# Summing w_mod products over the partitions on VectorE (32x32 transposes and row sums) instead of with matmuls against ones

## The chip, the cores and the metric

The kernel runs on one core of one Trainium2 chip. The metric is the device time of one execution in microseconds; lower is better. A core has a matmul engine (TensorE, PE in the profile), a vector engine (VectorE, DVE), an activation engine (ScalarE, ACT), GpSimd (POOL) and a queue that issues most of the transfers (SP). The engines run side by side and wait for one another by semaphores. On-chip memory has 128 partitions; VectorE works along a row of each partition, and a matmul sums over the partitions.

## What is computed

One transformer block: linear attention (32 heads of 32) and a gated feed-forward part, both behind a layer norm that is modulated by a vector `c`. Cut to what matters here:

```
mod = silu(c) @ w_mod                      # c: 1024 values, w_mod: 1024 x 6144, bf16
sa, ca, ga, sb, cb, gb = six slices of 1024 of mod
h = layernorm(x) * (1 + ca) + sa
x = x + ga * A(h, wqkv, wo)                # linear attention, x is 2048 x 1024
h = layernorm(x) * (1 + cb) + sb
x = x + gb * (gelu(h @ w_gate) * (h @ w_up)) @ w_down
```

The change touches `ga` (gate of the attention), `sb` and `cb` (shift and scale of the second layer norm) and `gb` (gate of the feed-forward part): 4 x 1024 values. `sa` and `ca` are made in another way at the start and stay as they are.

## The kernel before

**Stages.** The program builds a list of operations for each engine in program order. In the profile, the first 26 us load data and make the first layer norm; to 127 us the k and q products run (L919, L970); from 127 to 192 us 24 tiles of the attention's summary matrix ("m tiles", L934, 16 matmuls each, 2.32 us a tile); to some 255 us the output projection (L1304); then the feed-forward part (L1475) to 601 us and its down projection (L1688) to the end.

**Order.** PE and SP run in the order in which the program is written. For the operations between the last k products of the first chunks and the second layer norm (about 27 to 205 us), a planner, `reorder`, gives DVE, ACT and POOL an order of their own: it takes a cost for each operation from the table `COST` (duration and latency, by name), works a due time back from what needs the result, and fills each engine with the ready operation that is due first. The resulting order is fixed when the program runs; each engine waits for its next operation's inputs, whatever else would be ready.

**The w_mod products.** Slices of 512 columns are handled one after another, k = 0 to 7: 0 and 1 are `ga`, 2 to 5 are `sb` and `cb`, 6 and 7 are `gb`. For each, DVE multiplies eight blocks of 128 rows of w_mod by the matching values of silu(c) and adds them up (`mod_acc`, L855 and L858; `gb_acc`, L833 and L835): one accumulator of 128 x 512 f32. Slices alternate between two accumulators; 6 shares the one of 0, 2 and 4. What is left is a sum over the 128 partitions:

- `mod_hi` (ACT, L864 and L842) rounds the accumulator to bf16, `mod_lo` (DVE, L868 and L843) takes the difference to the unrounded value, also in bf16;
- `mod_rows` (PE, L880, shown in the profile as L879) multiplies both parts by a block of ones, 128 x 32, in eight matmuls, four column groups side by side, and adds them in PSUM;
- `mod_store` (ACT, L886) copies the row to on-chip memory, and SP stores it to a scratch row in DRAM (L888): four packets;
- SP loads it back where it is needed: `ga` to all partitions (`gab`, L894), which DVE then folds into W_o (`wofold`, L1241); `sb` and `cb` as columns (`sbT`, `cbT`, L1252); `gb` to all partitions much later.

`ga_pass` does this behind m tile 0, `mod_pass` behind tile 14, `gb_rows` behind tile 21.

**What stands around it.** Behind certain m tiles the program inserts the next steps (`HOOK`): `kv_prod` (PE, L952, eight short matmuls, then DVE's masked copy `kvt`, L956), which needs a DMA transpose `mtb<-mb` of the finished summary rows (`m_t`, L735, issued by SP); `w2_pair` (PE, L1235), which needs `kvt` and the folded W_o; `den` (PE, L1262), then on DVE an addition, a reciprocal and a cast (L1267 to L1269), a store on SP (L1271), loads (L1283) and the scaling of q (L1296). den0's store stands on SP behind the loads of `sbT` and `cbT` and ahead of the transpose for kv4.

Of the kernel before, what the change touches and what calls it, by code (L numbers as in the profile page):

```python
# [189 lines left out]
class Sched:  # L190
# [41 lines left out]
    def dma(self, stream, fn, rd=(), wr=(), deps=(), note="", overwrite_ok=False):  # L232
# [6 lines left out]
        if prev is not None:  # L239
# [11 lines left out]
        DVE_: {"min": (0.34, 0.085), "add": (0.607, 0.085), "bn": (0.603, 0.085), "aggr": (0.124, 0.085), "ve": (0.07, 0.085), "xhat": (0.46, 0.085),  # L251
               "nm": (0.074, 0.085), "hmod": (0.25, 0.085), "macc": (0.66, 0.085), "mlo": (0.6, 0.085), "kvt": (0.21, 0.085), "z": (0.34, 0.085),
               "dene": (0.335, 0.085), "rden": (1.67, 0.085), "pqs": (0.62, 0.085), "wofold": (1.13, 0.085), "x": (1.14, 0.085), "ssum": (1.15, 0.085), "tsum": (1.15, 0.085), "padd": (0.62, 0.085), "yT": (0.62, 0.085)},
# [96 lines left out]
def bass_adaLN_cond__linear_attn_block__geglu_ffn__prompt_kernel(  # L350
# [18 lines left out]
    with ExitStack() as es:  # L369
# [6 lines left out]
        def at(name, shape, dty, off):  # L376
            return nc.alloc_sbuf_tensor_at(name, shape, dty, offset=ABASE + off, align_bytes=4)
# [44 lines left out]
        GBB = at("gbb", [P, D], f32, OFF_GBB)  # L422
        MROW = [at(f"mrow{i}", [P, 512], f32, OFF_ROW + i * 2048) for i in range(2)]
        MROW0 = at("mrowa", [P, 256], f32, XHO[2])
        WMG = [at(f"wmg{i}", [P, 4, 512], bf16, HBO[3] + i * 4096) for i in range(2)]
        MRG = at("mrg", [P, 256], f32, OFF_TMP + 4096)
        HLG = at("hlg", [P, 2, 2, 512], bf16, OFF_TMP)
        GAC = at("gacc", [P, 512], f32, OFF_TMP + 4096)
        ACC = [at(f"acc{i}", [P, 512], f32, OFF_ROW + i * 2048) for i in range(2)]
        HLO = OFF_WS + 16384  # L430
        HL = at("hl", [P, 4, 2, 512], bf16, HLO)
        KVT = at("kvt", [P, NG, P], bf16, OFF_KVT)
# [6 lines left out]
        for name, shape, dty, sz in [  # L439
            ("ident", [P, P], bf16, 256), ("bmask", [P, P], bf16, 256), ("bm32", [P, NG, NH], bf16, 512),   # L440
            ("z32", [P, NG, NH], bf16, 512), ("rdc", [P, SGW // 2], f32, 1024), ("rdh", [P, SGW // 2], bf16, 512),
            ("ones", [P, 32], bf16, 64), ("silf", [P, NDC], f32, 64),
            ("c8", [NDC, P], bf16, 256), ("cT", [P, NDC], f32, 64), ("chalf", [P, NDC], f32, 64),
            ("thc", [P, NDC], f32, 64), ("siluT", [P, NDC], bf16, 64), ("modt", [P, 16], f32, 64), ("add4", [P, 4], f32, 64),
            ("sbT", [P, NDC], f32, 64), ("cb1T", [P, NDC], f32, 64),
            ("cbT", [P, NDC], f32, 64), ("zcols", [P, NG], f32, 64), ("neghalf", [P, 1], f32, 64),
            ("st", [P, NCH, 12], f32, NCH * 48), ("mv", [P, NCH, 2], f32, NCH * 8),
            ("rs", [P, NCH], f32, 64), ("nm", [P, NCH], f32, 64), ("ve", [P, NCH], f32, 64),
        ]:
# [7 lines left out]
        ONES, SILF, C8, CT, CHALF, THC, SILUT = (_small[k] for k in ("ones", "silf", "c8", "cT", "chalf", "thc", "siluT"))  # L457
        SBT, CB1T, CBT, ZCOLS = (_small[k] for k in ("sbT", "cb1T", "cbT", "zcols"))
# [4 lines left out]
        def r_sm(name):  # L463
            return [(SMO[name], SMO[name] + SMSZ[name], name)]
# [69 lines left out]
        def r_wm(i, d0=0, d1=NDC):  # L534
            return [(MSO[i] + d0 * 1024, MSO[i] + d1 * 1024, f"wmst{i}")]

        def r_hl(k, h0, h1):
            return [(HLO + (2 * (k % 4) + h0) * 1024, HLO + (2 * (k % 4) + h1) * 1024, "hl")]

# [129 lines left out]
        sch.op(V, lambda e: e.tensor_copy(SILF[:, :], SILUT[:, :]), rd=r_sm("siluT"), wr=r_sm("silf"))  # L669
        sch.op(V, lambda e: e.memset(ONES[:, :], 1.0), wr=r_sm("ones"))  # L670

# [153 lines left out]

        def r_hlg(j, h):
            return [(OFF_TMP + (2 * j + h) * 1024, OFF_TMP + (2 * j + h + 1) * 1024, "hlg")]

        def gb_acc(j, dc):
# [9 lines left out]

        def gb_hilo(j):  # L840
            acc, rng = GA_[j]
            sch.op(A, lambda e: e.activation(HLG[:, j, 0, :], acc[:, :], ACTF.Copy), rd=rng, wr=r_hlg(j, 0), note=f"mhi{6 + j}")  # L842
            sch.op(V, lambda e: e.tensor_tensor(HLG[:, j, 1, :], acc[:, :], HLG[:, j, 0, :], ALU.subtract), rd=rng + r_hlg(j, 0), wr=r_hlg(j, 1), note=f"mlo{6 + j}")  # L843

        o_gb = [None]

        def gb_rows():
            mod_rows(((0, 2, 5, lambda j, h: (HLG[:, j, h, :], r_hlg(j, h))),))
            o_gb[0] = mod_store(2, 5, MRG, [(OFF_TMP + 4096, OFF_TMP + 5120, "mrg")], 2)

# [10 lines left out]

        def mod_hi(k):
            rng = r_2k(OFF_ROW + k % 2 * 2048, f"acc{k % 2}")
            sch.op(A, lambda e: e.activation(HL[:, k % 4, 0, :], ACC[k % 2][:, :], ACTF.Copy), rd=rng, wr=r_hl(k, 0, 1), note=f"mhi{k}")  # L864

        def mod_lo(k):
            rng = r_2k(OFF_ROW + k % 2 * 2048, f"acc{k % 2}")
            sch.op(V, lambda e: e.tensor_tensor(HL[:, k % 4, 1, :], ACC[k % 2][:, :], HL[:, k % 4, 0, :], ALU.subtract),  # L868
                   rd=rng + r_hl(k, 0, 1), wr=r_hl(k, 1, 2), note=f"mlo{k}")

        def mod_rows(parts):
            for k0, n, bank, src in parts:
                o = None
                w = n * P
                for h in range(2):
                    for j in range(4):
                        ap, rng = src(k0 + j * n // 4, h)
                        ap = ap[:, j * w % 512:j * w % 512 + w]
                        o = sch.op(T, lambda e, h=h, j=j, ap=ap, bank=bank, w=w: e.matmul(  # L879
                            ps_all[32 * j:32 * (j + 1), bank * 512:bank * 512 + w], ONES[:, :], ap, start=(h == 0), stop=(h == 1)),  # L880
                            rd=rng + r_sm("ones"), pwr=(pr(bank) if h == j == 0 else ()), note=f"modr{k0}.{h}.{j}")
                pset_writer(bank, o)

        def mod_store(n, bank, dst, rng, row):
            w = n * P
            sch.op(A, lambda e: e.activation(dst[:, 0:w], ps_all[:, bank * 512:bank * 512 + w], ACTF.Copy),  # L886
                   prd=pr(bank), wr=rng, note=f"mrow{row}")
            return sch.dma(Q, lambda e: e.dma_start(scr_row[row, 0:n, :].rearrange("a (h b) -> (a h) b", b=w), dst[0:128:32, 0:w]), rd=rng, note=f"mrow{row}.st")  # L888

        def hl_src(k, h):  # L890
            return HL[:, k % 4, h, :], r_hl(k, h, h + 1)

# [354 lines left out]
        def mod_pass():  # L1247
            assert mdone[0] >= 48 and not late
            mod_rows(((2, 4, 5, hl_src),))
            o_r = mod_store(4, 5, MROW[1], r_2k(OFF_ROW + 2048, "mrow1"), 1)  # L1250
            for dst, nt, a0 in ((SBT, "sbT", 0), (CBT, "cbT", 2)):
                sch.dma(Q, lambda e, dst=dst, a0=a0: e.dma_start(dst[:, :], scr_row[1, a0:a0 + 2, :].rearrange("a (b p) -> p (a b)", p=P)),  # L1252
                        wr=r_sm(nt), deps=[o_r], note=nt)

# [72 lines left out]
        def hook_run(f):  # L1327
# [754 lines left out]
```

## Time and profile before

| what | value |
|---|---|
| three runs | 784.52, 784.8, 785.14 us; median 784.8 |
| profiled execution | 784.59 us, of which the profile's span is 782.8 |
| PE busy | 771.0 us, 98% |
| DVE busy | 646.2 us, 83% |
| ACT busy | 352.7 us, 45% |
| granted PE clock | 1.0 in all forty slices |

The profile gives, for each engine, when it was busy; the chain of waits follows the work that ended last back from the end, step by step, to what released it. An engine that is busy for a large share of the span need not set the time: only the steps on the chain do.

| operation touched | engine, line | count | mean ns |
|---|---|---|---|
| round the accumulator to bf16 | ACT L864, L842 | 8 | 622 to 632 |
| difference, bf16 | DVE L868, L843 | 8 | 678 to 693 |
| matmul with ones, 512 columns | PE L879 | 8 | 385 |
| matmul with ones, 256 columns | PE L879 | 16 | 278 |
| row copy out of PSUM | ACT L886 | 3 | 378, 592, 383 |
| row store | SP L888 | 3 | issue 521 to 647 |

Matmuls are pipelined, so the mean time of one is longer than its distance from the next.

### The profile page before, as it was taken

What the parts mean: (1) busy time and instruction counts of PE and PEld (TensorE: products, weight loads), DVE (VectorE), ACT (ScalarE), POOL (GpSimd) and SP (SyncE); (2) the same over time, 40 slices, a digit from 0 to 9 for tenths busy, and PEclk for the clock granted to TensorE, in tenths of its full rate; (3) what the DMA queues carried; (4) which work ended last, traced back from release to release, by engine and by line L of the source; (5) the groups of instructions that cost most, each with busy time, mean ns of one, the idle gap of its engine ahead of it and who ended that gap; (6) DMA issues with size and microseconds to landing.
All of it is one profiled execution on the core that took longest, in us unless ns stands there. A gap on an engine that the chain in (4) does not pass through costs nothing.

```text
span 782.8 us, 11022 instructions
## 1 busy us (share of the span) xinstructions
PE 771.0 (98%) x3805; PEld 500.6 (64%) x3868; DVE 646.2 (83%) x1089; ACT 352.7 (45%) x584; POOL 47.9 (6%) x126
## 2 busy tenths in 40 slices
PE   7999999999999999999999999999999999999998
PEld 4444445666445677767676776767676576677765
DVE  6699989993498978897999989898899897676777
ACT  2497743333474576776554444444544111111111
POOL 2131300000230011101000000000000000000000
PEclk9999999999999999999999999999999999999999
DMA  9889749836597068748445465646545444344341
GB/s 283 255 171 247 162 100 247 219 70 115 134 256 189 28 192 251 213 124 186 125 120 166 131 201 190 198 119 193 153 116 149 157 133 158 117 141 140 110 139 36
DMA packets 210543, 125.93 MB, mean 161 GB/s; under 512 B 70444, under 2 KB 200116, under 8 KB 210488
## 3 DMA queue, kind: packets, MB, share of 16 engines
q1 hardware_dynamic: 210472, 125.23, 59.2%
q8 instruction: 31, 0.51, 0.3%
q14 instruction: 24, 0.20, 0.1%
q10 hardware_dynamic: 16, 0.00, 0.0%
HBM read 88.35 MB, written 23.22 MB: 143 GB/s over the span
## 4 chain that ended last, share of the span: by engine, by line
PE 94%; DMA 2%; SPq 2%; issue 1%; DVE 0%; ACT 0%; DVEq 0%
PE ps_all L1475 45%; PE ps_all L1688 23%; PE ps_all L970 7%; PE ps_all L1304 7%; PE ps_all L934 6%; PE ps_all L919 6%; DMA mtb<-mb 1%; SPq L632 1%; DMA wmq<-in_w_mod_dram 1%; SPq L637 1%; PE ps_all L952 0%; PE ps_all L1235 0%; PE ps_all L1262 0%; SPq L626 0%; DVE xall L1317 0%
## 5 line engine op out<-in xcount | busy, mean ns | idle before, releaser
L1475 PE MATMUL ps_all<-ss,tp 128*128 128x512 f32 x896 | 214.7, 396 | 0.0
L1475 PEld LDWEIGHTS ps_all<-ss,tp 128*128 128x128 f32 x896 | 168.1, 188 | 38.2 <-DVE ps_all L1487 0.6
L1688 PE MATMUL ps_all<-bt,xs 128*128 128x512 f32 x525 | 125.5, 396 | 0.1
L1688 PEld LDWEIGHTS ps_all<-bt,xs 128*128 128x128 f32 x525 | 98.5, 188 | 22.8 <-issue 0.5
L1487 DVE TENSOR_TENSOR ps_all<-ps_all,es 128x512 f32<-128x512 f32 x112 | 77.5, 696 | 38.6 <-PE ps_all L1475 35.9
L1492 ACT ACTIVATE ge<-ps_all 128x512 f32<-128x512 f32 x112 | 64.0, 597 | 89.1 <-DVE ps_all L1487 45.0
L1496 DVE TENSOR_TENSOR yr<-ge,ps_all 128x512 bf16<-128x512 f32 x112 | 73.9, 679 | 2.2 <-PE ps_all L1475 1.5
L1443 DVE TENSOR_TENSOR tp<-wt 128x512 fp32r<-128x512 bf16 x112 | 74.1, 683 | 1.1 <-DMA wt<-in_B_w_gate_dram 0.7
L1443 DVE TENSOR_TENSOR tp<-wt,tp 128x512 fp32r<-128x512 bf16 x112 | 74.0, 682 | 0.0
L970 PE MATMUL ps_all<-h1T,wq 128*128 128x512 bf16 x256 | 56.7, 379 | 0.0
L919 PE MATMUL ps_all<-wk,h1T 128*128 128x512 bf16 x239 | 55.3, 379 | 1.1 <-DMA wk<-in_A_wqkv_dram 0.5
L1304 PE MATMUL ps_all<-w,pq 128*128 128x512 bf16 x251 | 55.9, 379 | 0.4
L1688 PE MATMUL ps_all<-bx,yl 128*128 128x512 bf16 x225 | 55.2, 380 | 0.7
L1475 PE MATMUL ps_all<-ar,tp 128*128 128x512 f32 x224 | 55.3, 389 | 0.0
L908 ACT ACTIVATE eb<-ps_all 128x512 f32<-128x512 f32 x64 | 36.4, 593 | 36.9 <-PE ps_all L919 15.3
L1475 PE MATMUL ps_all<-h20a,wt 128*128 128x512 bf16 x210 | 47.9, 379 | 0.9
L1475 PE MATMUL ps_all<-h21a,wt 128*128 128x512 bf16 x210 | 47.8, 379 | 0.9
L1475 PEld LDWEIGHTS ps_all<-ar,tp 128*128 128x128 f32 x224 | 42.0, 188 | 8.8
L1484 ACT ACTIVATE es<-ps_all 128x512 f32<-128x512 f32 x56 | 33.4, 599 | 30.8 <-PE ps_all L1475 30.8
L1481 ACT ACTIVATE ps_all<-ps_all 128x512 f32<-128x512 f32 x56 | 32.6, 582 | 31.2 <-PE ps_all L1475 30.9
L970 PEld LDWEIGHTS ps_all<-h1T,wq 128*128 128x128 bf16 x256 | 25.0, 98 | 29.9
L1304 PEld LDWEIGHTS ps_all<-w,pq 128*128 128x128 bf16 x256 | 24.7, 98 | 30.3 <-issue 0.5
(151 smaller groups left out, 889.4 us busy)
## 6 DMA issues: line engine op xcount, KB each, us to landing
wt<-in_B_w_gate_dram SPq DMA_DIRECT2D x28, 512.0 KB, 4.0
wt<-in_B_w_up_dram SPq DMA_DIRECT2D x28, 512.0 KB, 5.5
scr_y<-yr SPq DMA_DIRECT2D x56, 256.0 KB, 4.9
yl<-scr_y SPq DMA_DIRECT2D x8, 896.0 KB, 4.8
yl<-scr_y SPq DMA_DIRECT2D x14, 448.0 KB, 4.6
wmst<-in_w_mod_dram SPq DMA_DIRECT2D x6, 1024.0 KB, 5.6
wmq<-in_w_mod_dram SPq DMA_DIRECT2D x8, 512.0 KB, 6.0
rb<-scr_rd SPq DMA_DIRECT2D x32, 128.0 KB, 3.0
```

Source lines behind the costliest of these rows:

```text
L908: sch.op(A, lambda e: e.activation(EB[i][:, :], PS(bank), ACTF.Exp), prd=pr(bank), wr=rng, note=f"{note}.exp")
L919: o = sch.op(T, lambda e, dc=dc: e.matmul(PS(bank), H1[sg][:, ci, dc, :], W_[:, dc, jg * 512:(jg + 1) * 512], start=(dc == 0), stop=(dc == ...
L934: o = sch.op(T, lambda e, c_=c_: e.matmul(PS(bank, 0, n), PK[c_][:, g * P:(g + 1) * P], xrow(c_, o_, o_ + n), start=(c_ == 0), stop=(c_ == ...
L970: o = sch.op(T, lambda e, dc=dc: e.matmul(PS(b), WQ[:, dc, qc * P:(qc + 1) * P], H1[sg][:, :, dc, :], start=(dc == 0), stop=(dc == NDC - 1 ...
L1304: last[half] = sch.op(T, lambda e, g=g, half=half: e.matmul(PS(b0 + half), PQ[sg][:, g, ci * P:(ci + 1) * P], W2[:, g, half * 512:(half + ...
L1443: sch.op(V, lambda e, t=t: e.tensor_tensor(TP[k][:, t, :, :], in0[:, t, :, :], in1[:, t, :, :], ALU.subtract), rd=r0[t:t + 1] + (r1[t:t + ...
L1475: o = sch.op(T, lambda e, l_=l_, r_=r_, dc=dc: e.matmul(PS(b), l_, r_, start=fresh and dc == 0, stop=dc == ND2 - 1, skip_group_check=True) ...
L1484: sch.op(A, lambda e: e.activation(ES[t][:, :], PS(be + t), ACTF.Copy), prd=pr(be + t), wr=r_2k(OFF_ES[t], f"es{t}"), note="escp")
L1487: sch.op(V, lambda e: e.tensor_tensor(PS(dst + t), PS(BB + t), ES[t][:, :], ALU.add), prd=pr(BB + t), rd=r_2k(OFF_ES[t], f"es{t}"), pwr=pr ...
L1492: sch.op(A, lambda e: e.activation(GE[i][:, :], PS(b), ACTF.Gelu_apprx_tanh), prd=pr(b), wr=r_2k(OFF_GE[i], f"ge{i}"), note="gelu")
L1496: sch.op(V, lambda e: e.tensor_tensor(YR[:, 2 * (v % 2) + l, h * SGW:(h + 1) * SGW], GE[i][:, :], PS(b + 1), ALU.mult), rd=r_2k(OFF_GE[i], ...
L1688: pend_ = sch.op(T, lambda e, l_=l_, r_=r_, i=i: e.matmul(PS(b, c0, c1), l_, r_, start=fresh and i == 0, stop=i == n - 1, skip_group_check ...
```

## The change

The products stay. The sum over the partitions is made on DVE, in two steps.

`part_sum(k)`, once for each slice: a transpose of every 32x32 block of the accumulator (128 x 512 f32), then a sum along each run of 32 elements. The result has 16 values in each partition, the sum over one quarter of the partitions (32 of them). The sums of two slices, 1024 values in four quarters, stand side by side in one row of a small tile, `RDV`.

`mod_row(v, ...)`, once for each pair of slices: four copies bring the four quarters (partitions 0, 32, 64, 96 onward) side by side into partitions 0 to 31, a sum over the four, and a 32x32 transpose that puts the values in the order of the row. SP stores it with 32 packets of 32 values. `sb` and `cb` are now two such rows with two stores; both use the same three small tiles, and both loads wait for both stores.

The rounding copies on ACT, the differences on DVE, the matmuls with ones, the copies out of PSUM and the block of ones go. The planner's table gets costs for the new operations. Loads of the rows stay as they were.

```diff
+               "mtr": (0.6, 0.085), "mred": (0.6, 0.085), "qcp": (0.07, 0.085), "qred": (0.15, 0.085), "qtr": (0.08, 0.085),
...
+        TRO = [OFF_WS + 16384, OFF_WS + 18432]
+        RDO, QSO, QRO, QTO = (OFF_WS + 20480 + i * 512 for i in range(4))
+        TR = [at(f"tr{i}", [P, 512], f32, TRO[i]) for i in range(2)]
+        RDV = at("rdv", [P, 4, NH], f32, RDO)
+        QS = at("qs", [P, HPG, NH], f32, QSO)
+        QR = at("qr", [P, NH], f32, QRO)
+        QT = at("qt", [P, NH], f32, QTO)
...
+        def part_sum(k):
+            acc, rng = GA_[k - 6] if k >= 6 else (ACC[k % 2], r_2k(OFF_ROW + k % 2 * 2048, f"acc{k % 2}"))
+            i = k % 2
+            rt = r_2k(TRO[i], f"tr{i}")
+            sch.op(V, lambda e: e.transpose(TR[i][:, :], acc[:, :]), rd=rng, wr=rt, note=f"mtr{k}")
+            sch.op(V, lambda e: e.tensor_reduce(RDV[:, k // 2, i * 16:i * 16 + 16], TR[i][:, :].rearrange("p (a b) -> p a b", b=32), mybir.AxisListType.X, ALU.add),
+                   rd=rt, wr=r_rd(k), note=f"mred{k}")
+
+        def mod_row(v, row, a0):
...
+            for q in range(HPG):
+                sch.op(V, lambda e, q=q: e.tensor_copy(QS[0:32, q, :], RDV[32 * q:32 * (q + 1), v, :]), rd=r_rd(2 * v, 2), wr=[(QSO + q * 128, QSO + (q + 1) * 128, "qs")], note=f"qcp{v}.{q}")
+            sch.op(V, lambda e: e.tensor_reduce(QR[0:32, :], QS[0:32, :, :].rearrange("p q a -> p a q"), mybir.AxisListType.X, ALU.add), rd=rq, wr=rr, note=f"qred{v}")
+            sch.op(V, lambda e: e.transpose(QT[0:32, :], QR[0:32, :]), rd=rr, wr=rt, note=f"qtr{v}")
+            return lambda: sch.dma(Q, lambda e: e.dma_start(scr_row[row, a0:a0 + 2, :].rearrange("a (h i) -> (a h) i", i=32), QT[0:32, :]), rd=rt, note=f"mrow{v}.st")
...
                 gb_acc(j, dc)
                 if dc == NDC - 1:
-                    gb_hilo(j)
+                    part_sum(6 + j)
...
                 if dc == NDC - 1:
-                    late.setdefault(mblk[0] + 1, []).append(lambda k=k: mod_hi(k))
-                    late.setdefault(mblk[0] + 2, []).append(lambda k=k: mod_lo(k))
+                    late.setdefault(mblk[0] + 1, []).append(lambda k=k: part_sum(k))
...
         def ga_pass():
-            b = 6
-            mod_rows(((0, 2, b, hl_src),))
-            o_r = mod_store(2, b, MROW0, [(XHO[2], XHO[2] + 1024, "mrow0")], 0)
-            row_load(GAB, R_GAB, 0, 0, "gab", o_r)
+            row_load(GAB, R_GAB, 0, 0, "gab", mod_row(0, 0, 0)())
...
         def mod_pass():
             assert mdone[0] >= 48 and not late
-            mod_rows(((2, 4, 5, hl_src),))
-            o_r = mod_store(4, 5, MROW[1], r_2k(OFF_ROW + 2048, "mrow1"), 1)
+            o_r = [mod_row(v, 1, 2 * v - 2)() for v in (1, 2)]
...
-                gb_rows()
+                o_gb[0] = mod_row(3, 2, 0)()
```

More of the change, by code (lines that the diff above doesn't have):

```diff
@@ L422, in bass_adaLN_cond__linear_attn_block__geglu_ffn__prompt_kernel @@
         GBB = at("gbb", [P, D], f32, OFF_GBB)
-        MROW = [at(f"mrow{i}", [P, 512], f32, OFF_ROW + i * 2048) for i in range(2)]
-        MROW0 = at("mrowa", [P, 256], f32, XHO[2])
         WMG = [at(f"wmg{i}", [P, 4, 512], bf16, HBO[3] + i * 4096) for i in range(2)]
-        MRG = at("mrg", [P, 256], f32, OFF_TMP + 4096)
-        HLG = at("hlg", [P, 2, 2, 512], bf16, OFF_TMP)
         GAC = at("gacc", [P, 512], f32, OFF_TMP + 4096)
         ACC = [at(f"acc{i}", [P, 512], f32, OFF_ROW + i * 2048) for i in range(2)]
-        HLO = OFF_WS + 16384
-        HL = at("hl", [P, 4, 2, 512], bf16, HLO)
+        TRO = [OFF_WS + 16384, OFF_WS + 18432]
[5 more added lines that the diff above has]
+        QT = at("qt", [P, NH], f32, QTO)
         KVT = at("kvt", [P, NG, P], bf16, OFF_KVT)
@@ L441, in bass_adaLN_cond__linear_attn_block__geglu_ffn__prompt_kernel @@
             ("z32", [P, NG, NH], bf16, 512), ("rdc", [P, SGW // 2], f32, 1024), ("rdh", [P, SGW // 2], bf16, 512),
-            ("ones", [P, 32], bf16, 64), ("silf", [P, NDC], f32, 64),
+            ("silf", [P, NDC], f32, 64),
             ("c8", [NDC, P], bf16, 256), ("cT", [P, NDC], f32, 64), ("chalf", [P, NDC], f32, 64),
@@ L456, in bass_adaLN_cond__linear_attn_block__geglu_ffn__prompt_kernel @@
         RDC, RDH = _small["rdc"], _small["rdh"]
-        ONES, SILF, C8, CT, CHALF, THC, SILUT = (_small[k] for k in ("ones", "silf", "c8", "cT", "chalf", "thc", "siluT"))
+        SILF, C8, CT, CHALF, THC, SILUT = (_small[k] for k in ("silf", "c8", "cT", "chalf", "thc", "siluT"))
         SBT, CB1T, CBT, ZCOLS = (_small[k] for k in ("sbT", "cb1T", "cbT", "zcols"))
@@ L669, in bass_adaLN_cond__linear_attn_block__geglu_ffn__prompt_kernel @@
         sch.op(V, lambda e: e.tensor_copy(SILF[:, :], SILUT[:, :]), rd=r_sm("siluT"), wr=r_sm("silf"))
-        sch.op(V, lambda e: e.memset(ONES[:, :], 1.0), wr=r_sm("ones"))
         def ln_stats(c_, tag):
@@ L838, in gb_acc @@
                 gb_load(1, dc // 4)
[L840 to L843, printed above, removed]
         o_gb = [None]
-        def gb_rows():
-            mod_rows(((0, 2, 5, lambda j, h: (HLG[:, j, h, :], r_hlg(j, h))),))
-            o_gb[0] = mod_store(2, 5, MRG, [(OFF_TMP + 4096, OFF_TMP + 5120, "mrg")], 2)
         def mod_acc(k, dc):
@@ L871, in mod_rows @@
[L871 to L891, printed above, removed]
+        def r_rd(k, n=1):
+            return [(RDO + k * 64, RDO + (k + n) * 64, "rdv")]
@@ new lines, in mod_row @@
+        def mod_row(v, row, a0):
+            rq, rr, rt = ([(o_, o_ + w, n)] for o_, w, n in ((QSO, 512, "qs"), (QRO, 128, "qr"), (QTO, 128, "qt")))
+            for q in range(HPG):
[3 more added lines that the diff above has]
+            return lambda: sch.dma(Q, lambda e: e.dma_start(scr_row[row, a0:a0 + 2, :].rearrange("a (h i) -> (a h) i", i=32), QT[0:32, :]), rd=rt, note=f"mrow{v}.st")
```

15 lines of the change are left out of this document (2 added, 13 removed).

## The prediction

> **What bounds the kernel now.** I read the page first, then the chain of waits, then the stretches from 120 to 200 us (the three places that change lie there), and then the SP queue and VectorE (DVE) in order of time.
>
> ```profile
> PE 771.0 (98%) x3805; PEld 500.6 (64%) x3868; DVE 646.2 (83%) x1089; ACT 352.7 (45%) x584; POOL 47.9 (6%) x126
> PE 94%; DMA 2%; SPq 2%; issue 1%; DVE 0%; ACT 0%; DVEq 0%
> ```
>
> TensorE (PE) is the chain from 26 us on, so a microsecond of PE that is removed counts in full unless PE then waits for something else; a microsecond of another engine counts only where PE waits for it.
>
> ```profile
> 129.50 0.33 PE ps_all L879 x8
> 142.13 9.99 DMA mtb<-mb
> 152.16 0.62 PE ps_all L952 x8
> 165.71 0.55 PE ps_all L879 x8
> 179.94 0.55 PE ps_all L952 x8
> 186.66 0.33 PE ps_all L879 x8
> ```
>
> The chain in order of time (start, us, what). The three L879 pieces are all that the removed matmuls hold of PE. Between them stand two places where PE waits for a DMA transpose: kv1 at 152.16 and kv4 at 179.94 (the eight kv matmuls of L952, normally 0.45 long).
>
> ```profile
> 120.00:140.00 20.00, 20.00 (x129) 11.56 (x127) 17.48 (x32) 6.81 (x15) 0.00 (x0) 1.00 0.95 238
> 140.00:160.00 20.00, 19.46 (x141) 12.94 (x142) 19.82 (x27) 5.88 (x12) 0.00 (x0) 1.00 0.72 179
> 160.00:180.00 20.00, 19.89 (x175) 12.87 (x175) 16.25 (x26) 7.51 (x18) 0.00 (x0) 1.00 0.40 91
> 190.00:200.00 10.00, 9.95 (x64) 5.47 (x63) 0.78 (x3) 2.29 (x3) 0.00 (x0) 1.00 0.67 144
> ```
>
> Columns: PE, weight loads, DVE, ACT and POOL busy, the clock, the DMA share, GB/s. PE runs at the full clock. DVE is full from 140 to 160, has 3.75 us free from 160 to 180 and is nearly idle from 190 to 200: work added to it disappears by 200, but not necessarily before the dates in between. ACT is under 40% busy.
>
> ```profile
> 167.64 0.54 SPq L888 DMA_DIRECT2D scr_row<-mrow  x1
> 170.77 0.37 SPq L1252 DMA_DIRECT2D sbT<-scr_row  x1
> 171.20 0.57 SPq L1252 DMA_DIRECT2D cbT<-scr_row  x1
> 176.30 0.33 SPq L1271 DMA_DIRECT2D scr_rd<-rdh  x1
> 176.75 1.26 SPq L735 DMA_TRANSPOSE mtb<-mb  x1
> ```
>
> This is the date that matters. SP issues in program order: the row store, the two loads that wait for it, the store of the first reciprocal (den0), then the transpose mT4 that kv4 waits for. Before, SP is free at 171.77 and waits 4.5 us for den0's last DVE step (175.99, 0.29 long). kv4 runs at 179.87, the weight load in front of it having waited 0.28 for mT4: mT4's issue to kv4 takes 3.1 us and has no slack.
>
> ```profile
> 172.76 0.42 DVE L1267 TENSOR_SCALAR rdc<-ps_all 128x256 f32<-128x256 f32 x1 [1.03 <-PE ps_all L934]
> 173.76 1.75 DVE L1268 RECIPROCAL rdc<-rdc 128x256 f32<-128x256 f32 x1
> 175.99 0.29 DVE L1269 CAST rdh<-rdc 128x256 bf16<-128x256 f32 x1
> ```
>
> So PE's den0 (ends at 172.4), three DVE steps, a store and a transpose form a loop back to PE.
>
> **What is removed.** PE: 0.33 + 0.55 + 0.33 = 1.21 us. The m tile behind the second and the third takes 2.43 instead of 2.32 in the chain, 0.2 more: 1.4 gross. ACT: eight rounded copies of 0.63 and three row copies of 0.38, 0.59 and 0.38, together 6.4 us; nothing on the path, since ACT is 25 to 40% busy there and the tile evacuations beside them wait for PE. DVE: eight subtractions, 0.60 each from start to start (two in 1.20 from 118.43), 4.8 us. The memset of ones is at the start and hidden by the wait for weights.
>
> **What is added, all on DVE and SP.** Eight 32x32 transposes of 128x512 f32 and eight row sums of the same size; neither is in the trace. Nearest from below: the f32 tensor_scalar of 128x512 (L909), 0.42 long and 0.33 from start to start; from the middle: the 128x512 tensor_tensor, 0.68 and 0.60; from above: a 128x1024 operation, 1.22 and 1.14, as if f32 went at half rate. The shape is that of the middle row and I take it: the row sum reads what the transpose wrote and so waits for its full 0.68; 0.68 + 0.60 = 1.28 a pair, 10.2 us for eight (7.4 if the transpose goes like L909; 14.6 if it goes at half rate and the sum waits too).
>
> The Trainium skill's page "VectorE: DVE Perf Modes" (the perf-mode tier table and the rules for kernel authors) speaks against this step: it has tensor_reduce at one element a cycle in every type and calls it the slowest VectorE operation on a hot path. By that rule the low end for the sum falls away and 1.28 a pair stands; no run here shows it yet.
>
> Each of four mod_rows: four 32-partition copies, a sum over 128 elements, a transpose of 32 columns. Small operations in the trace last 0.14 to 0.17 (128x8 f32: 0.166) but follow one another at 0.06 where nothing holds them (36.86 to 36.92); the 128x128 kvt lasts 0.29. I take 4 x 0.17 + 0.29 + 0.20 = 1.17, because each later step reads the earlier one; low 4 x 0.07 + 0.20 + 0.15 = 0.63. Four: 4.7 us (2.5 to 4.7).
>
> The same page (two Vector instructions with no wait between them) says that an operation whose input starts in another quadrant than that of the last one is held until all before it are done. By this rule the four copies, which read four quadrants, go at the full 0.17; without it at 0.07, which would make three rows 1.2 us cheaper up to the critical store.
>
> DVE net: 10.2 + 4.7 - 4.8 = +10.1 us (5 to 14.5).
>
> **Where this lands.** Only the part ahead of the w_mod row for the second LN counts: six pairs instead of six subtractions, 6 x 0.68 = 4.1, and three mod_rows, 3.5: +7.6. DVE's idle time from 117 to 140 (1.23, 0.35, 1.04, 1.10) takes some 2.5 of it. The planner gives earlier due times to this chain, since two stores now stand in SP's line; the folds of W_o for the groups that w2 needs only from 192 on (three of 1.13) can move behind it, so +1.7 to +5.1 remains. Before, the products it queues behind end at 167.0; with the z mask and a kvt that go first (0.6), the last mod_row ends at 169.3 to 172.7, say 171.0.
>
> **SP.** mod_pass now issues two stores of 32 packets of 128 B instead of one of four of 2 KB. Both read one tile, so the second mod_row's transpose waits until the first store has landed, 3.1 us after issue by the 167.64 row (2.6 of it waiting). Behind that transpose stands all of DVE. The planner knows the latency and places other work between; I cost it at nothing, covered by the last products and sums; without that cover it is up to 3 us. The second store at 171.1 lands at 174.2, sbT and cbT take 0.43 + 0.57, and SP is free at 175.2: still ahead of den0's store at 176.3, with a margin of 1.1 us (0.45 if PE is 0.66 early). The gate rows' stores stay one each: the first is no longer held by ACT until 130.40 but stands behind 2 MB of W_o loads (issued 126.4 to 128.1) that hold the DMA engines until about 135 either way, so gab and the folds come no earlier; the third, at 188.55 before, may slip 4 us before mT7 (192.76) feels it.
>
> **The sum.** First place: 0.33 won at 129.5, lost at 152.16, where kv1 waits for a transpose that lands behind 3 MB of weights (issued 142.13, 10 us): 0. Second: 0.55 + 0.1 won; the den0 loop moves forward with PE, except that DVE no longer idles 1.03 before den0's first step, so that step waits for what runs then, up to 0.68: I take 0.4 off, 0.25 is left. Third: 0.33 + 0.1 = 0.43, nothing behind it. Together -0.7. The profiled execution took 784.59 (span 782.8 and 1.8 around it): 783.9; it lies 0.2 under the median of 784.8, so **784.1**. Own range 783.4 (both later savings kept, -1.1, and a little scatter) to 785.1.
>
> **Rivals.**
> 1. *The second store makes mT4 late* (slower). Point from which it decides: the second row store issued after about 172. Then each microsecond comes out at kv4 and at the end. With transposes at half rate, 6 x 0.54 = 3.2 later: store 174.3, SP free 178.4, den0's store and mT4 at 179.3, kv4 at 182.4 instead of 179.87: +2.5, less 0.43, is +2.1: **786.9**; a wait of DVE for the first store gives the same, both together 789. For it: DVE 99% busy from 140 to 160, no slack at kv4. Against: 4.5 us of SP waiting in that place before.
> 2. *kvt1 late* (slower). kvt1 ends at 156.25 and w2 needs it at 157.49: 1.24 us. If DVE is 2.5 us behind its plan there, PE loses 1.3, and the sum is **785.4**. Against: the planner places kvt by due time.
> 3. *All is kept* (faster). The row store lands earlier, kv1's wait goes too (0.55) and kv4's (0.28): 1.4 + 0.8 = 2.2: **782.6**. Against: the 2 MB ahead of the store.
> 4. The change doing nothing on PE can be left out: L879 goes.
>
> **Chances.** Forecast 0.46, first rival 0.34, second 0.10, third 0.10. A measurement of this kernel tells about 0.2% (1.6 us) from no change: faster is under 783.2, slower over 786.4. Faster: the third rival and a tail, 0.12. Slower: the first rival without its mild end and a bit of the second, with DVE's high prices, 0.36. Same: 0.52. The range of 783.0 to 787.6 leaves out the worst of the first rival and the best of the third.
>
> **What would show it.** No L879, and three tiles of the chain closing up; the transpose and the sum at 0.6 to 0.7 each; kv1 still at about 152.1; SP free before den0's store, and kv4 at about 179.6. Wrong: a row store on SP after 172 with PE idle ahead of kv4; a DVE wait for a row store; PE idle ahead of w2's second pair.

## The result, and the profile after

| | before | after |
|---|---|---|
| median of nine runs each | 785.1 us (784.52 to 785.64) | 787.29 us (786.71 to 787.8) |
| ratio, 95% interval | | 1.0030 [1.0021, 1.0038] |
| span of the profiled execution | 782.8 us | 785.4 us |

The change makes the kernel slower by some 2.2 us, 0.3%. The page after, busy times and the chain's shares by engine:

```profile
PE 769.7 (98%) x3781; PEld 500.4 (64%) x3844; DVE 654.6 (83%) x1120; ACT 347.5 (44%) x573; POOL 46.9 (6%) x126
PE 90%; DVE 5%; SPq 2%; DMA 1%; issue 1%; DVEq 0%
```

PE's busy time fell by 1.3 us, about what the three L879 groups held (1.21), and ACT's by 5.2. DVE's rose by 8.4, and DVE, which had 0% of the chain before, now has 5%: the chain runs through it. The first thing to find out is where. The stretches of the span after the change (PE, weight loads, DVE, ACT and POOL busy, the clock, the DMA share, GB/s):

```profile
120.00:140.00 20.00, 20.00 (x122) 11.73 (x121) 19.84 (x40) 5.38 (x12) 0.00 (x0) 1.00 1.00 236
140.00:160.00 20.00, 17.25 (x126) 11.40 (x127) 19.66 (x32) 4.42 (x10) 0.00 (x0) 1.00 0.76 188
160.00:180.00 20.00, 19.89 (x169) 13.37 (x170) 19.84 (x38) 6.47 (x14) 0.00 (x0) 1.00 0.32 68
180.00:190.00 10.00, 8.66 (x89) 5.71 (x88) 7.36 (x16) 2.19 (x4) 0.00 (x0) 1.00 0.83 165
190.00:200.00 10.00, 9.95 (x68) 5.94 (x68) 1.65 (x4) 2.11 (x4) 0.00 (x0) 1.00 0.46 98
```

DVE is now full from 120 to 180 (59.34 of 60 us; before 53.55). PE has two holes: 2.75 us between 140 and 160, 1.34 between 180 and 190. Before, the first stretch had 0.54 and the second 0.05:

```profile
180.00:190.00 10.00, 9.95 (x108) 6.65 (x108) 5.20 (x9) 3.21 (x6) 0.00 (x0) 1.00 0.77 132
```

From 190 to 200 PE is as busy as before (9.95 of 10). PE's waits between 120 and 200 (who waits, for what: us in total, times, longest), and the three places in order of time, the wait in brackets:

```profile
PE ps_all L925 <- DMA mtb<-mb: 2.2, 2, 1.3
PE ps_all L1204 <- DVE kvt L929: 1.8, 1, 1.8
...
152.78 0.62 PE L925 MATMUL ps_all<-mtb,wv 128*128 128x128 bf16 x8 [0.92 <-DMA mtb<-mb]
159.82 0.38 PE L1204 MATMUL ps_all<-wo,kvt 128*128 128x512 bf16 x1 [1.77 <-DVE kvt L929]
...
182.92 0.62 PE L925 MATMUL ps_all<-mtb,wv 128*128 128x128 bf16 x8 [1.29 <-DMA mtb<-mb]
```

These are kv1, the second pair of w2 and kv4 (L952, L1235 and L952 of the kernel before). "w2" below is this second pair. Before, kv1 waited 0.44, w2 not at all, and the weight load ahead of kv4 0.28.

One measure is used from here on: the **m stage**, from the start of the first m tile to the start of the output projection. It leaves out how late the k and q products end, which differs by up to 1.4 us from run to run. Before it was 127.02 to 192.46 = 65.44, after 127.59 to 195.07 = 67.48: +2.04, nearly the whole loss. It adds up piece by piece, each taken from the start of one group to the start of the next:

| piece of the m stage | before | after | difference |
|---|---|---|---|
| first m tile to kv1 | 25.14 | 25.19 | +0.05 |
| kv1 to w2 | 5.33 | 7.04 | +1.71 |
| w2 to den0 | 13.89 | 13.24 | -0.65 |
| den0 to kv4 | 8.49 | 9.86 | +1.37 |
| kv4 to the output projection | 12.59 | 12.15 | -0.44 |

PE wins where the second and the third group were. What it wins at the first group it gives back at kv1. It loses at w2 and at kv4.

**Why w2 waits.** DVE in order of time, after:

```profile
139.26 0.69 DVE L854 STREAM_TRANSPOSE tr<-acc 128x512 f32<-128x512 f32 x1
...
140.19 0.66 DVE L855 TENSOR_REDUCE rdv<-tr 128x16 f32<-128x512 f32 x1
...
141.38 0.76 DVE L861 COPY qs<-rdv 32x32 f32<-32x32 f32 x4
142.17 0.37 DVE L862 TENSOR_REDUCE qr<-qs 32x32 f32<-32x128 f32 x1
142.57 0.20 DVE L863 STREAM_TRANSPOSE qt<-qr 32x32 f32<-32x32 f32 x1
142.71 3.44 DVE L1210 TENSOR_TENSOR wo<-wo,gab 128x1024 bf16<-128x1024 bf16 x3
...
158.65 0.70 DVE L854 STREAM_TRANSPOSE tr<-acc 128x512 f32<-128x512 f32 x1
159.28 0.25 DVE L929 TENSOR_TENSOR kvt<-ps_all,bmask 128x128 bf16<-128x128 f32 x1
```

And the same places before:

```profile
139.98 5.76 DVE L1241 TENSOR_TENSOR wo<-wo,gab 128x1024 bf16<-128x1024 bf16 x5 [1.10 <-DMA gab<-scr_row]
...
155.97 0.28 DVE L956 TENSOR_TENSOR kvt<-ps_all,bmask 128x128 bf16<-128x128 f32 x1
```

The folds of W_o (L1210, L1241 before) start at 142.71; before, at 139.98, where DVE had idled 1.10 for `gab`. From there to `kvt1` both kernels run the same list: all eight folds, `kvt0`, ten products. Before it took 15.99 us; after, a transpose (158.65) stands ahead of `kvt1` too, and it takes 16.57. So `kvt1` runs at 159.28, not 155.97: 2.73 of the 3.31 us because the sums of slices 0 to 3 and the two rows made of them run ahead of the folds, 0.6 for the transpose. Its input has been there since kv1 ended at 153.4. PE wanted it at 158.05.

**Why kv4 waits.** PE's den0, before and after, and then DVE and SP after:

```profile
171.38 1.06 PE L1262 MATMUL ps_all<-pq,z 128*32 128x256 bf16 x32
```

```profile
173.06 1.06 PE L1230 MATMUL ps_all<-pq,z 128*32 128x256 bf16 x32
```

```profile
174.43 0.16 DVE L863 STREAM_TRANSPOSE qt<-qr 32x32 f32<-32x32 f32 x1
...
175.74 0.40 DVE L1235 TENSOR_SCALAR rdc<-ps_all 128x256 f32<-128x256 f32 x1
...
176.73 1.73 DVE L1236 RECIPROCAL rdc<-rdc 128x256 f32<-128x256 f32 x1
...
178.97 0.27 DVE L1237 CAST rdh<-rdc 128x256 bf16<-128x256 f32 x1
```

```profile
169.26 5.68 SPq L864 DMA_DIRECT2D scr_row<-qt  x2
175.99 0.38 SPq L1220 DMA_DIRECT2D sbT<-scr_row  x1
176.42 0.58 SPq L1220 DMA_DIRECT2D cbT<-scr_row  x1
179.31 0.34 SPq L1239 DMA_DIRECT2D scr_rd<-rdh  x1
179.76 1.24 SPq L732 DMA_TRANSPOSE mtb<-mb  x1
```

PE's den0 began at 173.06 (before 171.38), and its store went at 179.31 (176.30): from one to the other 6.25 us, where it had been 4.92. There is no idle on DVE in between: den0's first step stands behind `qt`, a product and a row sum. SP is free at 177.0 and then waits 2.3 us for DVE's cast; the second row store is late (174.5), but it's not what SP waits for in the end. The transpose follows the store by 0.45, as before, and kv4 follows that by 3.16 (3.12 before). So of the 1.37 us from den0 to kv4, 1.33 lie between den0 and its store.

That is a reading of one trace. Whether these two places are the cause, and whether the second store has a part in it, had to be tried.

### The profile page after: what moved, and what is told of

Same layout as the page of the kernel before. It is cut to its first block, busy times and chain, and to the rows that moved or that the text cites. A ratio compares the mean times of both kernels' runs of the same rounds, so it can differ in the third digit from the quotient of the medians.

```text
span 785.4 us, 10997 instructions
## 1 busy us (share of the span) xinstructions
PE 769.7 (98%) x3781; PEld 500.4 (64%) x3844; DVE 654.6 (83%) x1120; ACT 347.5 (44%) x573; POOL 46.9 (6%) x126
## 4 chain that ended last, share of the span: by engine, by line
PE 90%; DVE 5%; SPq 2%; DMA 1%; issue 1%; DVEq 0%
PE ps_all L1443 44%; PE ps_all L1656 23%; PE ps_all L1272 7%; PE ps_all L943 6%; PE ps_all L892 6%; PE ps_all L907 3%; DVE acc L843 2%; DVE wo L1210 1%; DMA wmq<-in_w_mod_dram 1%; SPq L630 1%; SPq L635 1%; DVE pq L884 0%; DMA mtb<-mb 0%; PE ps_all L925 0%; PE ps_all L1204 0%
```

## The experiments

All ratios are to the kernel before, run beside them on the same chip, with a 95% interval. Theory A, in short: DVE is late at `kvt1` and at den0, and PE pays there. Theory B is the prediction's first rival, the second store on SP. The "theory C" that stands in the expectation of e1 takes each wait of PE for itself. Rival C of e8 to e11 is another: every microsecond of work added on DVE costs its share, whatever the order. Rival D comes with e9.

Four kernels keep all of the change and move operations within DVE's fixed order. A helper was added behind the planner's call; `move(names, ahead_of)` takes operations out of DVE's list and puts them back ahead of a named one. `macc k.d` is product d of slice k, `mtr`/`mred` a slice's transpose and sum, `z32` the mask for den, `dene0`, `rden0`, `rdenh0` den0's three steps.

```diff
+        def move(names, ahead_of):
+            l = sch.streams[DVE_]
+            ops = [next(o for o in l if o.note == n) for n in names]
+            for o in ops:
+                l.remove(o)
+            k = next(i for i, o in enumerate(l) if o.note == ahead_of)
+            l[k:k] = ops
...
```

**e1: kvt1 ahead.**

```diff
+        move(("kvt1",), "macc4.4")
```

> Theory A (VectorE is late and its fixed order holds kvt1 and den0's three steps behind w_mod work): with kvt1 four products earlier, the 1.8 us that PE waits ahead of w2's second pair goes, but kv4 still waits for den0's steps, which stay at the same place in VectorE's line: kv4's wait grows from 1.3 to some 3 us and the time stays at 787.3, within 0.5. Theory B (the second row store holds SP, and with it mT4): kv4 is bound by the store, the same 787.3. Theory C (each PE wait counts by itself): 785.5.

Measured: 787.62 us, 1.0028 [1.0017, 1.0039], as theories A and B said; theory C's 785.5 falls. PE's waits in this kernel:

```profile
PE ps_all L925 <- DMA mtb<-mb: 3.0, 2, 1.5
PE ps_all L1230 <- DVE z L1198: 1.1, 1, 1.1
```

The wait for `kvt1` is gone, and the time is the same. But kv4's wait did not grow to the some 3 us of theory A: PE now waits 1.12 for the z mask 13 us later, and 1.44 at kv4: den0's store goes at 179.24 (179.31 without the move), for DVE's list ahead of it is as long as it was. kv1 waits 1.52 in this run, 0.92 in the changed kernel. A wait that is taken away ahead of a second, later limit gives nothing.

**e2: den0's steps ahead.**

```diff
+        move(("macc7.2", "mtr6", "macc7.3", "mred6", "macc7.4", "macc7.5"), "macc7.6")
```

> den0's addition, reciprocal and cast ahead of six products and sums of the last gate, kvt1 left where it is. Theory A: PE's wait ahead of kv4 (1.3 us) goes, kvt1's 1.8 stays: 786.0. Theory B (SP is held by the second store): the den0 store leaves no earlier than the stores and loads ahead of it allow, and kv4 is as late as before: 787.3.

Measured: 787.11 us, 1.0022 [1.0013, 1.0031]; theory A had said 786.0. SP and PE around kv4:

```profile
177.98 1.24 SPq L732 DMA_TRANSPOSE mtb<-mb  x1
```

```profile
182.93 0.62 PE L925 MATMUL ps_all<-mtb,wv 128*128 128x128 bf16 x8 [0.82 <-DMA mtb<-mb]
```

den0's store goes at 177.53, 1.8 earlier, and kv4 runs at 182.93 as in the changed kernel (182.92): its transpose, issued at 177.98, took 4.95 us to kv4 instead of 3.16. In this run `gab` came 2 us later, PE waited 1.66 at kv1 and 1.0 at kv0, the latter for nothing that the profile shows. What den0 won was not seen at the end.

**e3: both, with the last gate's products behind.**

```diff
+        move(("kvt1",), "macc4.4")
+        move(("z32",), "mred4")
+        move(("macc7.0", "macc7.1", "macc7.2", "mtr6", "macc7.3", "mred6", "macc7.4", "macc7.5"), "macc7.6")
```

> kvt1, the z mask and den0's steps all ahead. Theory A: both waits go, 1.8 + 1.1: 784.4, some 0.7 below the kernel before (PE's three groups of matmuls gone, kv1's wait kept). Theory B: kv4 stays held by the store, gain at most 0.5 over the changed kernel: 786.8.

Measured: 786.99 us, 1.0018 [1.0009, 1.0027]; theory A had said 784.4, theory B 786.8. The ratio is 0.0012 under that of the change, and the two intervals overlap, so it isn't shown that any of the loss is back. kv1 waits 1.64, kv4 0.71 (its transpose takes 4.8), and a w2 pair 0.81 for `kvt4`, which now stands behind the last gate's products.

**e4: a tile of its own for the second row**, so that its last transpose doesn't wait for the first store.

```diff
+        QT2 = at("qt2", [P, NH], f32, QTO + 512)
...
+            QT_ = QT2 if v == 2 else QT
...
-            sch.op(V, lambda e: e.transpose(QT[0:32, :], QR[0:32, :]), rd=rr, wr=rt, note=f"qtr{v}")
+            sch.op(V, lambda e: e.transpose(QT_[0:32, :], QR[0:32, :]), rd=rr, wr=rt, note=f"qtr{v}")
...
+        own = next(o for o in sch.streams[DVE_] if o.note == "qtr2")
+        own.deps = [d for d in own.deps if d.note != "mrow1.st"]
+        move(("qtr2",), "z32")
```

> The second row of sb and cb has a tile of its own for its last transpose, which moves ahead of the z mask; all else in the changed kernel's order. SP's two row stores and the loads behind them leave some 1.5 us earlier. Theory A: den0's store waits for the cast on VectorE anyway: 787.3, within 0.4. Theory B: kv4 comes 1.3 us earlier: 786.0.

Measured: 787.77 us, 1.0029 [1.0017, 1.0042]. SP in this kernel:

```profile
174.08 0.38 SPq L1222 DMA_DIRECT2D sbT<-scr_row  x1
174.51 0.58 SPq L1222 DMA_DIRECT2D cbT<-scr_row  x1
179.19 0.34 SPq L1241 DMA_DIRECT2D scr_rd<-rdh  x1
```

SP is free at 175.1, 1.9 us earlier, and den0's store goes within 0.12 us of where it went. The second store takes no part in kv4's wait: theory B falls.

**c1: the kernel before, once more.**

> The kernel before, unchanged, beside itself: a ratio of 1.000 within 0.001 under every theory, and a second profile of it: kv1's wait (0.44 us in the first) and the landing of the first gate's row (5.0 us after its issue) show how much these move by themselves.

Measured: 785.39 us, 1.0002 [0.9993, 1.0011]. Its trace is worth more than its time:

```profile
152.80 0.62 PE L952 MATMUL ps_all<-mtb,wv 128*128 128x128 bf16 x8 [1.32 <-DMA mtb<-mb]
```

kv1 waits 1.32 here, 0.44 in the first profile, and the m stage is 66.33 against 65.44. So kv1's wait moves by 0.9 from one execution to the next of the same kernel, and a difference of less than that at kv1 can't be put down to the change.

What it moves with stands on SP. The load of `gab` waits there for the first gate's row store, and the loads and the transpose for kv1 stand behind it. In all twelve traces in which that store stands behind the W_o loads (before, c1, the changed kernel, e1 to e6, e9 to e11) kv1 runs 16.8 to 17.2 us after the load of `gab` is issued, and that date moves by 1.9 us within the m stage. In e7 and e8, where the load comes 4 to 7 us earlier, PE no longer waits at kv1.

**e5: the planner's prices put right.** The table has 0.51 for a row (4 x 0.07 + 0.15 + 0.08), the trace 1.3.

```diff
-"qcp": (0.07, 0.085), "qred": (0.15, 0.085), "qtr": (0.08, 0.085)
+"qcp": (0.19, 0.085), "qred": (0.33, 0.085), "qtr": (0.17, 0.085)
```

> The planner's table gets the measured prices of the small steps (copy 0.19, sum 0.33, last transpose 0.17 instead of 0.07, 0.15, 0.08); nothing else. kvt1 then stands ahead of one transpose, two small steps go behind the first folds, and den0's addition ahead of one product and one sum. Theory A (VectorE late, order): some 1.2 us of the two waits come back, 786.0. If the order does not matter: 787.3.

Measured: 787.62 us, 1.0032 [1.0020, 1.0044]. The order is shuffled, w2 still waits 1.69 for `kvt1` and 0.84 for `kvt0`, kv4 1.22. Theory A had said 786.0. `kvt1` stands ahead of a transpose in this order, but it runs no earlier, 31.98 us into the m stage against 31.69 in the changed kernel: all eight folds are still ahead of it. The wrong prices are not the cause.

**e6: the same instructions, small.** The transposes and sums read 32 of the 512 columns, and the table has 0.1 for them; the rest of each sum is left out.

```diff
-            sch.op(V, lambda e: e.transpose(TR[i][:, :], acc[:, :]), rd=rng, wr=rt, note=f"mtr{k}")
+            sch.op(V, lambda e: e.transpose(TR[i][:, 0:32], acc[:, 0:32]), rd=rng, wr=rt, note=f"mtr{k}")
```

> The transposes and row sums work on 32 columns instead of 512 (15 of 16 columns of each accumulator are left out of the modulation), with a price of 0.1 in the table: VectorE gets less work than before the change, all else as changed. Theory A: the waits ahead of w2's second pair and kv4 go and the saved matmuls show: 784.3, 0.8 below the kernel before. If the stores, the packets or SP make the change slow: 786.5 or more.

Measured: 786.09 us, 1.0013 [1.0003, 1.0022]. Theory A had said 784.3. PE waits for no DVE result any more; the waits left are 1.65 at kv1 and 1.30 at kv4. About half of the loss went with DVE's work. The rest did not. den0's store follows den0 by 4.97 us (172.00 to 176.97), as it did before the change, but the transpose behind it took 4.45. Over all traces it took from 3.1 to 5.0, the longest in e2, e3 and e6. Why was not found: the traffic around it differs in each, and in e2 the DMA engines moved 2 GB/s from 180 to 181 us, with the transpose still under way.

**e7: the first gate's row ahead of the loads of W_o, and DVE in the order that PE needs.** The true prices of e5, too.

```diff
+        o_ga = mod_row(0, 0, 0)()
         wo_load(0)
         wo_load(1)
...
-            row_load(GAB, R_GAB, 0, 0, "gab", mod_row(0, 0, 0)())
+            row_load(GAB, R_GAB, 0, 0, "gab", o_ga)
...
+        move(("kvt1",), "macc4.4")
+        move(("z32",), "mred4")
+        move(("wofold 6", "wofold 7"), "kvt5")
+        move(("qtr2",), "macc7.1")
+        move(("mtr6", "macc7.2", "mred6", "macc7.3", "macc7.4"), "macc7.5")
+        move(("kvt4",), "mtr7")
```

> The changed kernel with the true prices, the first gate's row stored ahead of the two loads of W_o, kvt1, kvt4, the z mask and den0's steps ahead in VectorE's order, and the last two folds of W_o moved to where VectorE was idle (190 to 193 us). Theory A: no wait of PE but kv1's, and that one short, since gab and one slice of w_mod load earlier: 783.4, 1.7 below the kernel before. If DMA luck decides kv1: 784.3.

Measured: 785.41 us, 1.0001 [0.9993, 1.0010]: all of the loss is back, though theory A had said 783.4. What is left of PE's waits:

```profile
169.27 0.61 PE L925 MATMUL ps_all<-mtb,wv 128*128 128x128 bf16 x8 [1.13 <-DMA mtb<-mb]
181.25 0.62 PE L925 MATMUL ps_all<-mtb,wv 128*128 128x128 bf16 x8 [0.55 <-DMA mtb<-mb]
```

kv1 doesn't wait. kv3 does, because its transpose stands on SP behind a load of w_mod that waited for a product of the last gate (164.26, then 164.73).

**e8: those two taken on as well.** The early row and the true prices of e7 stay, and this list of moves stands in place of that of e7. `move` takes an engine's list as its last argument here; the second row has its own tile as in e4.

```diff
+        move(("kvt1",), "macc4.4")
+        move(("wofold 6", "wofold 7"), "kvt5")
+        move(("z32",), "macc6.7")
+        move(("qcp2.0", "qcp2.1", "qcp2.2", "qcp2.3", "qred2", "qtr2", "kvt3"), "macc7.0")
+        move(("dene0", "rden0", "rdenh0"), "macc7.0")
+        move(("kvt4",), "mtr7")
+        move(("mT3",), "wmg1.0", SP_)
```

> e7 with its two remaining waits of PE taken on. The transpose for kv3 goes ahead of a w_mod load on SP (it stood behind it and PE waited 1.13 us), the second row has a tile of its own (VectorE idled 1.55 us for the first store), and the second row and den0's three steps go ahead of the products for the last slice. Theory A (PE loses only where a VectorE result or a transpose behind one is late, so in the right order nothing of the change costs PE anything): the waits of e7, 1.13 and 0.55 us, go, and the time comes out 0.5 to 1.7 us under before, ratio 0.998 to 0.9995. Rival C (added work on VectorE comes out somewhere whatever the order): 1.000 to 1.003, with a new wait of PE for VectorE.

Measured: 783.57 us against 785.23 before, 0.9982 [0.9973, 0.9991]. It beats both kernels. Its stretches:

```profile
140.00:160.00 20.00, 20.00 (x152) 13.57 (x151) 19.77 (x34) 5.54 (x12) 0.00 (x0) 1.00 0.72 170
160.00:180.00 20.00, 20.00 (x197) 13.37 (x194) 18.98 (x35) 5.62 (x14) 0.00 (x0) 1.00 0.48 97
180.00:190.00 10.00, 10.00 (x84) 6.64 (x73) 9.70 (x19) 2.39 (x4) 0.00 (x0) 1.00 0.49 108
```

PE is busy without a gap from 120 to 200, with the same work on DVE as in the changed kernel (654.6 us in both): 19.77 of 20 us from 140 to 160, 9.70 of 10 from 180 to 190, and no matmul waits for it. den0's three steps now run as one block, and the store and the transpose are 5 us ahead of where the changed kernel has them:

```profile
171.51 0.42 DVE L1237 TENSOR_SCALAR rdc<-ps_all 128x256 f32<-128x256 f32 x1 [0.54 <-PE ps_all L909]
171.97 1.75 DVE L1238 RECIPROCAL rdc<-rdc 128x256 f32<-128x256 f32 x1
173.76 0.29 DVE L1239 CAST rdh<-rdc 128x256 bf16<-128x256 f32 x1
```

```profile
174.12 0.44 SPq L1241 DMA_DIRECT2D scr_rd<-rdh  x1
174.67 1.24 SPq L733 DMA_TRANSPOSE mtb<-mb  x1
```

The m stage is 63.46. It had 65.00 in the kernel before without its wait at kv1; the difference of 1.54 is what PE gains when nothing is given back. It fits the pieces above: 0.65 and 0.44, and 0.43 for the first group. e8 orders DVE anew and moves a store and a transpose on SP, so it shows that the added work need not cost anything, not what each move is worth. How much of e8's gain the kernel before would have from a better order of its own was not tried.

**e9 to e11: one part of the change alone**, in the kernel before. The sums of some slices are made on DVE as in the change, the others by matmuls with ones.

```diff
-                    late.setdefault(mblk[0] + 1, []).append(lambda k=k: mod_hi(k))
-                    late.setdefault(mblk[0] + 2, []).append(lambda k=k: mod_lo(k))
+                    if k in (0, 1):
+                        late.setdefault(mblk[0] + 1, []).append(lambda k=k: part_sum(k))
+                    else:
+                        late.setdefault(mblk[0] + 1, []).append(lambda k=k: mod_hi(k))
+                        late.setdefault(mblk[0] + 2, []).append(lambda k=k: mod_lo(k))
```

This is e9, with `ga_pass` as in the change; e10 has (2, 3, 4, 5) and the changed `mod_pass`; e11 has `part_sum(6 + j)` for `gb_hilo(j)` and `mod_row` for `gb_rows`. All three have one tile for the transposed slices, where the change has two.

> The kernel before, with the partition sums of the first gate alone (slices 0 and 1) made on VectorE. VectorE gets 2 x 1.28 + 1.3 - 1.2 = 2.7 us more, all ahead of kvt1, with some 2.5 us of idle before 140 to take it; PE loses the first group (0.33 us). Theory A: kvt1 is late by at most a few tenths beyond its 1.24 us of slack, kv4 is untouched: -0.3 to +0.5 us, ratio 0.9996 to 1.0006. Rival D (the 32-packet store behind the loads of W_o is what costs): kv1 waits 1 us more and the ratio is 1.001 or more. Rival C (cost in proportion to the work added, 2.2 us for 10): +0.6 us, 1.0008.

> The kernel before, with the sums for the second norm alone (slices 2 to 5) made on VectorE: 4 x 1.28 + 2 x 1.3 - 2.4 = 5.3 us more, some 2.6 of it ahead of kvt1 and all of it ahead of den0's first step; PE loses the middle group (0.55 us). Theory A: w2's second pair waits 0.3 to 1.5 us for kvt1 and kv4 waits about 1 us for its transpose: +0.7 to +2.0 us, ratio 1.001 to 1.0025. Rival C: +1.2 us, 1.0015, which lies inside; the trace tells them apart by where PE waits.

> The kernel before, with the sums of the last gate alone (slices 6 and 7) made on VectorE: 2.7 us more, of which one pair (1.28 less the 0.60 of the difference) stands ahead of den0's first step, where VectorE idled 1.03 us, and the rest lies from 180 to 190, where it has room. PE loses the last group (0.33 us). Theory A: nothing is late, -0.2 to -0.5 us, ratio 0.9993 to 0.9998. Rival C: +0.6 us, 1.0008.

| part alone | median (before 785.23) | ratio, 95% | m stage (65.44 and 66.33 before) | PE waits for |
|---|---|---|---|---|
| e9, first gate | 785.64 us | 1.0003 [0.9995, 1.0012] | 65.76 | kv1 1.21 |
| e10, second norm | 786.96 us | 1.0019 [1.0010, 1.0028] | 67.18 | below |
| e11, last gate | 785.03 us | 0.9996 [0.9987, 1.0004] | 65.33 | kv1 0.75 |

PE's waits in e10:

```profile
158.24 0.60 PE L1264 MATMUL ps_all<-wo,kvt 128*128 128x512 bf16 x2 [1.14 <-DVE kvt L982]
172.10 1.06 PE L1290 MATMUL ps_all<-pq,z 128*32 128x256 bf16 x32 [0.33 <-DVE z L1258]
181.63 0.62 PE L978 MATMUL ps_all<-mtb,wv 128*128 128x128 bf16 x8 [0.96 <-DMA mtb<-mb]
```

The second norm's part loses clearly, and its trace shows the same two places. Its den0's store follows den0 by 5.94 us (172.10 to 178.04), 1.02 more than before, and its transpose took 3.14. The parts add up to 0.0018 against the whole's 0.0030, with some 0.0009 of uncertainty on each. All three came out as theory A said. Rival C (so many us on DVE, so many at the end) said 1.0008 for the last gate; it got 0.9996 [0.9987, 1.0004], and e8 has all of the work and none of the cost. Rival D (the 32-packet store behind the loads of W_o) wanted 1.001 or more from e9. It got 1.0003, but 1.001 lies inside the interval, and kv1's wait of 1.21 lies between those of the two profiles before. So D is not needed, but a few tenths of a microsecond at kv1 are not excluded.

**What the eleven kernels show together.** Theory A's times came in for e1 and e8 to e11, and for e4 but for 0.1 us. They were too low by 1.1 to 2.6 us for e2, e3, e5, e6 and e7. In the traces of e2, e3 and e6 two transposes lie behind that, which the theory had taken as fixed: that of kv1, which moves with the first gate's store, and that of kv4, which took 4.4 to 5.0 us there. In e7 two waits are left, 1.13 at kv3 and 0.55 at kv4. So it is shown where the change loses its time, that DVE is late there, and that neither the second store nor the work as such is the cause. The one run that set den0's steps ahead and nothing else, e2, was not clearly shorter, so how much of the loss comes back at kv4 by DVE's order alone is not shown.

## Why the prediction was wrong

It said 784.1 us, no change; it is 787.29, slower. That this lies inside the range it gave, 783.0 to 787.6, is luck: the upper part stood there for the first rival, which isn't what happened. Its own steps, one by one:

- **What PE gains: right.** 1.4 gross; the second and the third place were put at 0.65 and 0.43 and gave 0.65 and 0.44, and e8, which gives nothing back, shows 1.54.
- **What DVE's operations cost: right.** 1.28 a pair: the transpose is 0.69, the sum 0.66, and 0.63 + 0.59 from start to start with other work between them, 0.74 + 0.72 back to back (180.72, 181.46, 182.18). A row was 1.17; it is 1.33 (141.38 to 142.71). DVE's busy time rose by 8.4, net, where 10.1 was said (5 to 14.5). The Trainium skill's page "VectorE: DVE Perf Modes" (the perf-mode tier table and the rules for kernel authors) calls tensor_reduce the slowest operation of VectorE; its rule of one element a cycle, by which the low price fell away, fits the trace: the sum of 512 elements takes 0.59 from start to start, and the tensor_scalar of that size 0.33. But the sum is no slower than the tensor_tensor of the same size (0.68, 0.60). What the same page of the Trainium skill says on two Vector instructions with no wait between them (the section of that name) fits the trace too, though no run tries the copies without a change of quadrant: the four copies from four quadrants last 0.16 to 0.17 each and take 0.76 together, where small operations followed one another at 0.06 elsewhere.
- **The first place, swallowed at kv1: right, but the number is luck.** kv1 came 25.19 us into the m stage, 25.14 before. In c1 it came at 26.03, so a single pair of profiles can't show it to a tenth.
- **Where DVE's work lands: wrong, and this is the step that failed.** The prediction let three folds of W_o move behind the second norm's row, so that DVE would be late by +1.7 to +5.1 at the last row only, and left `kvt1` on time. The planner did the reverse: the first of those two rows went ahead of the folds, all eight folds stayed ahead of `kvt1`, and it came 3.31 us late. That is the second rival, in mechanism and nearly in size (DVE 2.5 us behind, PE loses 1.3; measured 3.31 late, and 1.71 lost from kv1 to w2). The sum has no term for this place. It was given 0.10 because "the planner places kvt by due time". What its order shows is that the row and the folds were taken first, with the true prices too (e5).
- **den0's first step, "up to 0.68: I take 0.4 off": mis-sized.** It cost 1.37 from den0 to kv4. From den0 to its store took 6.25 us instead of 4.92, 1.33 more, since not one operation but several got between PE's result and the three steps. The term that is missing at w2 (1.71) and this one (1.37 for 0.4) make up the difference between the -0.7 that was forecast and the +2.04 of the m stage, but for 0.06.
- **SP: the dates were late, the conclusion was right.** The last row ended at 174.6 (171.0 was said), SP was free at 177.0 (175.2); den0's store went at 179.31 (176.3). The margin grew from 1.1 to 2.3, since DVE was later than SP. The first rival's price, 786.9, is nearest to the result, but that is chance: e4 refutes its mechanism, and its sum puts 0.9 us from SP free (178.4) to the transpose (179.3), where the rows it reads have 0.45.
- **The wait for the first store: right.** It cost nothing here, other work stood ahead of the second transpose. In e7, where that cover was moved, DVE idled 1.55 us for it.

What isn't settled: the 4.4 to 5.0 us that kv4's transpose took in e2, e3 and e6, and with it what is left of e6's loss; and how much the first gate's 32-packet store costs at kv1.

## What to carry to other kernels

Work that moves from an engine on the path to one that is off it is free only ahead of dates that someone has looked up: list what the receiving engine owes the path (here `kvt1`, the z mask and den0's steps), and count what the fixed order puts in front of each, not the free time of a stretch. Of two such dates, mending the first alone gives nothing if the second is set by the same queue (e1); with all of them in order, and two transfers moved ahead on SP, 8 us more of DVE's work cost nothing (e8). And before reading a difference of under 1 us at one wait, look at the same wait in a second profile of the unchanged kernel.

## What the hardware showed that wasn't expected

- kv1's wait for its transpose, which lands behind 3 MB of loads, was 0.44 and 1.32 us in two profiles of the same kernel. In twelve traces kv1 kept a distance of 16.8 to 17.2 us from the load of `gab`.
- The first gate's row store, 4 KB, was followed by the load that waits for it after 4.7 to 5.5 us with four packets (before, c1, e10, e11) and after 7.1 to 8.7 us with 32 packets (the changed kernel, e1 to e6, e9); all of them stand behind 2 MB of W_o loads. That is not the price of the packets alone: the 32 went out 1.8 to 2.3 us earlier in the m stage, and the load followed 8.0 to 8.9 us into the stage with four and 8.2 to 9.9 with 32. Issued ahead of those loads, the 32 packets took 3.7 (e8, 126.74 to 130.40) and 5.2 (e7, 127.08 to 132.28).
- The transpose for kv4 took 3.1 to 5.0 us from issue to kv4, with the same bytes.
